# A fused Fourier transform and MLP kernel: the order of the weight conversions in its first chunk, and two transform parts placed at earlier steps

## The chip, the cores and the metric

The kernel runs on one core of a Trainium2 chip. The metric is the time of one execution on the device in microseconds; the kernel before has a median of 988.9 us over three runs (988.49 to 988.94). A lower time is better.

The core has five engines, each with its own queue of instructions that it works through in order: TensorE (matmuls; PE in the profile, and PEld for its weight loads), VectorE (DVE), ScalarE (ACT), GpSimd (POOL) and SyncE (SP, which here only issues DMAs). An instruction waits at the head of its queue until what it needs is there, and everything behind it on that engine waits too.

## The reference

```python
def _attn_ref(x):                       # x: 8 x 3136 x 256
    X = np.fft.fft(x, axis=1)
    X = np.fft.fft(X, axis=2)
    return X.real.astype(np.float32)

def _moe_ref(x, g_ln, w_ch1, w_ch2):    # w_ch1: 256 x 1024, w_ch2: 1024 x 256
    mu = np.mean(x, axis=-1, keepdims=True)
    var = np.mean((x - mu) ** 2, axis=-1, keepdims=True)
    xn = (x - mu) / np.sqrt(var + 1e-06) * g_ln
    ch = np.maximum(xn @ w_ch1, 0.0) @ w_ch2
    return (x + ch).astype(np.float32)
```

The output is `_moe_ref(_attn_ref(x), ...)`: the real part of a two-dimensional Fourier transform, and on its rows a normalised two-layer MLP with a residual.

## The kernel before

The long transform (3136 points) is done as matmuls in two steps. Step 1 multiplies folded input with a 64-point table and stores the result to a scratch tensor in DRAM; step 2, `step2(m, part)`, reads it back in another layout and multiplies it with a second table. A batch has 8 such parts m, so there are 64 in all. Each part makes 196 columns (tokens) of transformed data; the tokens are cut into chunks c of 256. A chunk's data exist three times: in full (`ck`), as a rounded high half (`ckh`) and as the rest (`ckl`), since products are made from three passes of halves. `step2` has its parts named by letters: "m" the matmuls (L311) into a PSUM bank, "h" the cast to the high half on ScalarE (L332), "f" the full copy on ScalarE (L334), "l" the subtraction for the low half on VectorE (L336). The bank is the single bank "fft", or "y" where a second part falls on the same step.

The MLP runs in steps s, eight to a chunk (s = 8c + f, f being a slice of 128 of the 1024 hidden columns):

- `moe1_a(s)`: six matmuls (L356) of the slice of w1 with the chunk into a PSUM bank of the pair "ab", so that s uses the bank of s-2; then a copy on ScalarE (`asb`, L361) and two adds on VectorE (L362 and L363, `h`). The second add is the last reader of the bank.
- `moe1_b(s)`: on ScalarE the rectified high half (`h_hi`, L370), on VectorE the low half (`h_lo`, L371). `h_lo` needs `h_hi`.
- `moe2(s)`: twelve matmuls (L406) of `h_hi` and `h_lo` with w2's halves, summed over the chunk's eight steps.

The main loop issues for each s: `moe1_b(s-1)`, `moe1_a(s)`, what is listed under "late" for s, `moe2(s-3)`, and what is listed under "after" for s (step 2 and 1 parts, residuals, stores). So VectorE's and ScalarE's queues hold what is "late" for s right behind the adds or the copy of s, and TensorE's queue holds the "after" matmuls behind `moe2(s-3)`. A table made at L619 to L629 gives each step 2 part m its s: eight steps for each chunk in which the part's first token lies, less 3; its "l" part is late at s+1. The steps before s = 6 are written out by hand (L767 to L813), mixed with the preparation of the weights.

The weights arrive as 64-bit integers (doubles) and are converted to float32 on the engines. For tile n of w2 (four tiles of two hidden slices each): `convert_m` is two VectorE instructions (L523, L525), `convert_z` one on ScalarE (L531), `convert_b` two on VectorE (L536, L538; it needs `convert_z`), `finish_w2` one on VectorE (L598). `split_w2` then casts the high half on ScalarE (L542) and subtracts for the low half on GpSimd (L543). Tile n is needed by `moe2` of f = 2n and 2n+1. w1 goes through a matmul as well (L576); its high half is cast by `round_w1`, its rest computed by `rest_w1` (L589) and cast by `rest_w1_copy` (L594), for columns 0 to 511 with k = 0 and for 512 to 1023 (used by s = 4 to 7 of a chunk) with k = 1.

TensorE begins with some warm-up matmuls (L683), does step 1 of the first batch, the matmuls of w1, more warm-up, and then `step2(0)` and `step2(1)`; `moe1_a(0)` starts 34 us into the span.

Of the kernel before, what the change touches and what calls it, by code (L numbers as in the profile page):

```python
# [32 lines left out]
CW = 256  # L33
# [113 lines left out]
def tile_kernel(ctx: ExitStack, tc: tile.TileContext, x, g_ln, w1, w2, tu, tab, tz, ty, tw, out):  # L147
# [139 lines left out]
    def first_token(m):  # L287
        b, j = divmod(m, 8)
        return b * REG + max(gb[2 * j] - 2, 0)
# [212 lines left out]
    def convert_a(key, wp):  # L502
        convert_m(key, wp)
        convert_z(key, wp)
# [24 lines left out]
    def convert_z(key, wp):  # L529
        high, e = conv[key][:2] if key in conv else convert_e(key, wp)  # L530
        nc.scalar.activation(e, high.bitcast(F32), AF.Copy, scale=2.0 ** -112)  # L531
# [13 lines left out]
    w1p, w2p = [], []  # L545
# [26 lines left out]
    def transform_w1(k, i):  # L572
        for j in range(2):
            if i == 0:
                psw[k, j] = psum.tile([128, 512], F32, tag=f"acc{k}", name=f"psw{k}{j}", bufs=2)
            nc.tensor.matmul(psw[k, j], tw_s[:, i, j], gws[2 * k + i], start=(i == 0),  # L576
                             stop=(i == 1))
# [14 lines left out]
    def rest_w1_copy(k):  # L592
        for j in range(2):
            nc.scalar.copy(w1_cols(w1_lo, k, j), psw.pop((k, j)))  # L594

    def finish_w2(n):
        _, e, f = conv.pop(f"w2_{n}")
        nc.vector.scalar_tensor_tensor(out=f, in0=f, scalar=2.0 ** -20, in1=e, op0=ALU.mult,  # L598
                                       op1=ALU.mult)
        return f  # L600

    def split_w2(n, f):
        split(w2_hi[:, 2 * n:2 * n + 2], w2_lo[:, 2 * n:2 * n + 2],
              f.rearrange("p (f d) -> p f d", f=2), nc.gpsimd)
# [10 lines left out]
    def add_late(s, fn, *args):  # L615

        late.setdefault(s, []).append((fn, args))

    first = {}  # L619
    for m in range(3, 64):  # L620
        s = 8 * (first_token(m) // CW) - 3
        if s in first:
            second.add(m)
        first.setdefault(s, []).append(m)
    for s, ms in first.items():
        for m in ms:
            add(s, step2, m, "mhf")
        for m in ms:
            add_late(s + 1, step2, m, "l")  # L629
    def behind(s):  # L630

        return s + 1 + (len(first[s]) > 1)
# [46 lines left out]
    def warm_up(n, zeros):  # L679

        pw = psum.tile([128, 2 * D], F32, tag="fft", name="pw")
        for i in range(n):
            nc.tensor.matmul(pw, zeros[:, :128], zeros, start=True, stop=True)  # L683

    E = mybir.EngineType
    with tc.manual_schedule(engines={E.PE, E.Activation, E.DVE, E.Pool}):
        with tc.manual_schedule(engines={E.SP}):
            nc.vector.memset(one, 1.0)
            for t in (warm, warm_h):
                nc.vector.memset(t, 0.0)  # L690
            for n, t in ((2, warm), (3, warm_h)):
                warm_up(n, t)
            nc.scalar.dma_start(tu_s, tu)
            load_x(0, 0)
            nc.scalar.activation(one, one, AF.Sqrt)
            for i in range(1, 5):
                load_x(0, i)
            load_w1(0)
            for i in (5, 6):
                load_x(0, i)  # L700
            nc.scalar.dma_start(g_s, g_ln.rearrange("(i p) -> p i", p=128))
            load_w1(1)
            nc.sync.dma_start(tw_all, tw)
            load_w1(2)
            load_w1(3)
            nc.gpsimd.memset(zmu, 0.0)
            nc.gpsimd.memset(masked, 0.0)
            ends(0, 0, 6)
            for i in range(3):
                fold_zw(0, i, nc.vector)  # L710
                step1(0, i)
            step1_ends(0, 0, 6)
            for i in range(3):
                store1(0, i, nc.scalar if i % 2 else nc.gpsimd)
            fold_zw(0, 3, nc.vector)
            step1(0, 3)
            ends(0, 6, 10)
            fold_zw(0, 4, nc.vector)
            convert_z("w1_0", w1p[0])
            convert_m("w1_0", w1p[0])  # L720
            step1(0, 4)
            step1_ends(0, 6, 10)
            store1(0, 3, nc.scalar)
            store1(0, 4, nc.gpsimd)
            fold_zw(0, 5, nc.vector)
            convert_b("w1_0")
            step1(0, 5)
            ends(0, 10, NS)
            fold_zw(0, 6, nc.vector)
            convert_z("w1_1", w1p[1])  # L730
            nc.vector.tensor_scalar_mul(g_s, g_s, 2.0 ** -20)
            finish_w1(0)
            convert_m("w1_1", w1p[1])
            step1_ends(0, 10, NS)
            store1(0, 5, nc.scalar)
            convert_b("w1_1")
            convert_z("w1_2", w1p[2])
            finish_w1(1)
            step1(0, 6)
            store1(0, 6, nc.gpsimd)  # L740
            load_w2(0, nc.gpsimd)
            nc.gpsimd.dma_start(tab_s[:, :, :gb[4]], tab[:, :, :gb[4]])
            nc.gpsimd.dma_start(tz_s, tz)
            load_w2(1, nc.gpsimd)
            convert_z("w1_3", w1p[3])
            convert_m("w1_2", w1p[2])
            convert_b("w1_2")
            finish_w1(2)
            relayout(0, 0, 2)
            relayout(0, 2, 4)  # L750
            relayout(0, 4, 8)
            nc.sync.dma_start(tab_s[:, :, gb[4]:gb[8]], tab[:, :, gb[4]:gb[8]])
            load_w2(2)
            relayout(0, 8, 16)
            nc.scalar.copy(minus, tw_all[:, 512:])
            transform_w1(0, 0)
            transform_w1(0, 1)
            round_w1(0)
            convert_m("w1_3", w1p[3])
            convert_b("w1_3")  # L760
            load_w2(3)
            nc.sync.dma_start(ty_s, ty)
            nc.sync.dma_start(tab_s[:, :, gb[8]:], tab[:, :, gb[8]:])
            for i in range(NU):
                load_x(1, i)
            finish_w1(3)
            transform_w1(1, 0)  # L767
            rest_w1(0)
            rest_w1_copy(0)
            transform_w1(1, 1)  # L770
            round_w1(1)
            convert_z("w2_0", w2p[0])
            convert_m("w2_0", w2p[0])
            convert_b("w2_0")
            split_w2(0, finish_w2(0))
            convert_m("w2_1", w2p[1])
            warm_up(10, warm_h)
            step2(0, "m")
            step2(0, "hl")
            step2(1, "m")  # L780
            step2(1, "hl", 0)
            convert_z("w2_1", w2p[1])
            convert_b("w2_1")
            moe1_a(0, ((1, 0), (0, 0), (0, 1)))
            moe1_a(1, ((1, 0), (0, 0), (0, 1)))
            rest_w1(1)
            moe1_b(0)
            step2(0, "f")
            moe1_a(2)
            f = finish_w2(1)  # L790
            moe1_b(1)
            split_w2(1, f)
            moe1_b(2)
            moe1_a(3)
            rest_w1_copy(1)
            step2(1, "f")
            convert_a("w2_2", w2p[2])
            step2(1, "hl", 1)
            moe2(0)
            moe1_b(3)  # L800
            moe1_a(4)
            convert_b("w2_2")
            f = finish_w2(2)
            nc.gpsimd.tensor_scalar(out=neg, in0=ty_s[:, 1, 129:130], scalar1=2.0, scalar2=-1.0,
                                    op0=ALU.mult, op1=ALU.add)
            moe2(1)
            step2(2, "m")
            moe1_b(4)
            split_w2(2, f)
            moe1_a(5)  # L810
            step2(2, "hf")
            step2(2, "l")
            convert_a("w2_3", w2p[3])  # L813
            moe2(2)
            add_late(6, convert_b, "w2_3")
            add_late(6, lambda: w2f.append(finish_w2(3)))
            add_late(7, lambda: split_w2(3, w2f.pop()))
            add_late(14, split, t1_hi, t1_lo, tu_s[:, 0:128])

        main.append(True)  # L820
        lag, last = 3, 8 * NCH
        for s in range(6, last):
            moe1_b(s - 1)
            moe1_a(s)
            for fn, args in late.get(s, ()):
                fn(*args)
            moe2(s - lag)
            for fn, args in after.get(s, ()):
                fn(*args)
        moe1_b(last - 1)  # L830
        inverse_std(LC)
        moe2(last - 3)
        for i, side in ((0, 0), (1, 0), (0, 1), (1, 1)):
            for t in (last - 2, last - 1):
                moe2(t, ((i, side),))
            finish_last(i, side)
# [18 lines left out]
```

## Time and profile before

| | us |
|---|---|
| median of three runs | 988.9 |
| the profiled execution | 988.67 |
| its span (first to last instruction) | 986.9 |
| TensorE busy | 976.8 |
| VectorE busy | 815.5 |
| ScalarE busy | 535.6 |
| GpSimd busy | 252.1 |

The profile is one execution taken by the hardware profiler. In its lists of instructions in order of time a row has the start within the span, the duration, the engine, the line of the kernel, the operation, output<-inputs by the program's names (buffer numbers left out), the shape, the number of instructions, and in brackets the idle time of the engine ahead of it and what ended that. Matmuls overlap in the pipeline, so that one lasts 0.28 us while they start 0.11 us apart. In the list of waits a row has the waiting engine and its line, what it waited for, and the time in total, how often, and the longest.

### The profile page before, as it was taken

How to read it: one execution, taken by the hardware profiler on the slowest of the kernel's cores; microseconds unless marked ns; L12 is line 12 of the kernel's file. 1: busy time of each engine (PE TensorE's matmuls, PEld its weight loads, DVE VectorE, ACT ScalarE, POOL GpSimd, SP SyncE). 2: the span in 40 equal slices, each digit the busy share in tenths (PEclk: the TensorE clock that was granted, in tenths of full speed). 3: DMA queues.
4: the chain of work that ended last, by engine and by line, in shares of the span. 5: the costliest groups of instructions: out<-in, count | busy, mean ns of one | idle time of the engine just before them, and what ended most of it. 6: DMA issues, size and time to landing. Idle time of an engine off the chain costs nothing.

```text
span 986.9 us, 22042 instructions
## 1 busy us (share of the span) xinstructions
PE 976.8 (99%) x8426; PEld 962.9 (98%) x8427; DVE 815.5 (83%) x2190; ACT 535.6 (54%) x1416; POOL 252.1 (26%) x282
## 2 busy tenths in 40 slices
PE   9899999999999999999999999999999999999998
PEld 6699999999999999999999999999999999999998
DVE  6888887888888888878888888888888888888887
ACT  3655655555555555555555556555555554555553
POOL 3247343224322332322342234223322300000000
PEclk9999999999999999999999999999999999999999
DMA  8924352215221252112521242212311112100101
GB/s 336 330 101 134 101 173 76 87 54 150 76 97 55 75 161 87 65 65 73 164 86 54 86 139 87 96 55 75 109 52 36 54 53 88 44 23 22 44 23 44
DMA packets 41161, 92.12 MB, mean 93 GB/s; under 512 B 4080, under 2 KB 18400, under 8 KB 40160
## 3 DMA queue, kind: packets, MB, share of 16 engines
q1 hardware_dynamic: 39088, 87.25, 26.7%
q0 software_dynamic: 736, 2.47, 0.7%
q8 instruction: 67, 1.10, 0.5%
q10 hardware_dynamic: 1232, 0.99, 0.3%
q14 instruction: 38, 0.31, 0.1%
HBM read 50.32 MB, written 40.37 MB: 92 GB/s over the span
## 4 chain that ended last, share of the span: by engine, by line
PE 91%; DVE 7%; ACT 2%; issue 1%; ACTq 0%; DVEq 0%
PE acc L406 50%; PE ab L356 25%; PE ps L311 6%; PE psy L431 4%; PE ps L263 3%; DVE h_lo L371 2%; DVE h L362 1%; DVE h L363 1%; PE pw L683 1%; ACT h_hi L370 1%; DVE ew L538 0%; PE ps L255 0%; PE ps L257 0%; DVE fw L525 0%; DVE st L453 0%
## 5 line engine op out<-in xcount | busy, mean ns | idle before, releaser
L406 PE MATMUL acc<-w_hi,h_lo 128*128 128x256 f32 x1568 | 433.2, 276 | 0.2 <-DVE h_lo L371 0.2
L406 PE MATMUL acc<-w_hi,h_hi 128*128 128x256 f32 x1568 | 433.0, 276 | 0.0
L406 PE MATMUL acc<-w_lo,h_hi 128*128 128x256 f32 x1568 | 433.0, 276 | 0.0
L371 DVE SCALAR_TENSOR_TENSOR h_lo<-h,h_hi 128x512 fp32r<-128x512 f32 x392 | 294.1, 750 | 141.2 <-ACT h_hi L370 138.8
L370 ACT ACTIVATE h_hi<-h 128x512 fp32r<-128x512 f32 x392 | 250.0, 638 | 292.9 <-DVE h L363 292.9
L406 PEld LDWEIGHTS acc<-w_hi,h_lo 128*128 128x128 f32 x1568 | 294.3, 188 | 0.6 <-DVE h_lo L371 0.4
L406 PEld LDWEIGHTS acc<-w_hi,h_hi 128*128 128x128 f32 x1568 | 294.4, 188 | 0.0
L406 PEld LDWEIGHTS acc<-w_lo,h_hi 128*128 128x128 f32 x1568 | 294.4, 188 | 0.0
L356 PE MATMUL ab<-ckl,w_hi 128*128 128x256 f32 x768 | 218.0, 284 | 2.3 <-DVE h L363 2.3
L356 PE MATMUL ab<-ckh,w_lo 128*128 128x256 f32 x768 | 212.7, 277 | 2.0 <-ACT w_lo L594 1.7
L356 PE MATMUL ab<-ckh,w_hi 128*128 128x256 f32 x768 | 212.1, 276 | 0.0
L225 POOL TENSOR_TENSOR fl<-f,fh 128x512 fp32r<-128x512 f32 x49 | 64.0, 1306 | 504.9 <-ACT fh L219 494.2
L362 DVE TENSOR_TENSOR h<-asb,ab 128x256 f32<-128x256 f32 x384 | 158.7, 413 | 0.5 <-ACT asb L361 0.5
L363 DVE TENSOR_TENSOR h<-asb,ab 128x256 f32<-128x256 f32 x384 | 158.9, 414 | 0.0
L356 PEld LDWEIGHTS ab<-ckl,w_hi 128*128 128x128 f32 x768 | 144.2, 188 | 3.5 <-issue 1.9
L356 PEld LDWEIGHTS ab<-ckh,w_lo 128*128 128x128 f32 x768 | 144.3, 188 | 2.5 <-ACT w_lo L594 1.9
L356 PEld LDWEIGHTS ab<-ckh,w_hi 128*128 128x128 f32 x768 | 144.2, 188 | 0.0
L361 ACT COPY asb<-ab 128x256 f32<-128x256 f32 x384 | 137.9, 359 | 8.9 <-PE ab L356 1.2
L267 ACT COPY s<-ps 128x508 f32<-128x508 f32 x56 | 32.8, 586 | 62.6 <-PE ps L263 50.7
L311 PE MATMUL ps<-tab_s,s 112*128 112x98 f32 (+1 forms) x512 | 65.6, 273 | 0.1
L311 PEld LDWEIGHTS ps<-tab_s,s 112*128 112x128 f32 x512 | 61.8, 191 | 0.6 <-PE pw L683 0.6
L332 ACT CAST ckh<-ps 128x392 fp32r<-128x392 f32 (+49 forms) x112 | 39.7, 356 | 39.7 <-PE ps L311 39.5
(111 smaller groups left out, 980.2 us busy)
## 6 DMA issues: line engine op xcount, KB each, us to landing
xs<-x SPq DMA_DIRECT2D x56, 512.0 KB, 4.1
out<-o SPq DMA_DIRECT2D x96, 256.0 KB, 2.0
scratch<-s SPq DMA_DIRECT2D x49, 256.0 KB, 2.3
s<-scratch SPq DMA_DIRECT2D x7, 1792.0 KB, 9.8
w1p_all<-w SPq DMA_DIRECT2D x6, 512.0 KB, 8.9
scratch<-s POOLq DMA_DIRECT2D x4, 256.0 KB, 6.0
w1p_all<-w POOLq DMA_DIRECT2D x2, 512.0 KB, 5.2
s<-scratch SPq DMA_DIRECT2D x1, 896.0 KB, 10.9
```

The lines of the kernel that those rows point to most:

```text
L225: nc.gpsimd.tensor_tensor(out=lo, in0=f, in1=hi.bitcast(F32), op=ALU.subtract)
L267: nc.scalar.copy(s[:, :, :, :127], ps[:, :, :, :127])
L311: nc.tensor.matmul(ps[:, h, k0 - base:k1 - base], s2[b][:KP, g, 128 * h:128 * h + 128], tab_s[:, h, k0:k1], start=(h == 0 and g == 2 * j), ...
L332: nc.scalar.copy(hi, src)
L356: nc.tensor.matmul(pt, wt[wi][:, j, fs], ch[xi][:, j, :w], start=(n == 0), stop=(n == 2))
L361: nc.scalar.copy(asb[:, :w], pa)
L362: nc.vector.tensor_tensor(out=h[:, :w], in0=asb[:, :w], in1=pb, op=ALU.add)
L363: nc.vector.tensor_tensor(out=h[:, w:], in0=asb[:, :m], in1=pb[:, :m], op=ALU.subtract)
L370: nc.scalar.activation(h_hi, h, AF.Relu)
L371: nc.vector.scalar_tensor_tensor(out=h_lo, in0=h, scalar=0.0, in1=h_hi.bitcast(F32), op0=ALU.max, op1=ALU.subtract)
L406: nc.tensor.matmul(acc[c, i][:, side], hs[xi][:, h0:h0 + 128], ws[wi][:, f], start=(f == 0 and side == 0 and n == 0), stop=(f == 7 and n = ...
L431: nc.tensor.matmul(ps[:, j, :n], ck[:, j], ty_s[:, j, :n], start=(j == 0), stop=True, skip_group_check=True)
```

## The change

In the written-out part the conversions of w2's tiles are put in another order between the other work: `convert_z` of tile 0 ahead of `transform_w1(1, 1)` and `round_w1(1)`; all of tile 1's conversion ahead of `step2(0)`, its finish ahead of `moe1_a(0)` and its split behind it; tile 2 begun behind `moe1_b(0)`; the finish of tile 3 late at step 7 and no longer at 6. `rest_w1_copy(1)` goes ahead of `moe1_b(1)`, the full copies of step2(0) and step2(1) further back. In the table step2(3) goes from step 13 to 7 (its "l" part from 14 to 10), step2(4) from 21 to 10 (its "l" from 22 to 14). Step2(5) stays at 21; as it is alone there now, it uses bank "fft" and not "y". The instructions themselves and their number stay the same, and so does TensorE's order apart from the two moved parts.

```diff
@@ the table of step 2 parts
-        s = 8 * (first_token(m) // CW) - 3
+        s = {3: 7, 4: 10}.get(m, 8 * (first_token(m) // CW) - 3)
...
         for m in ms:
-            add_late(s + 1, step2, m, "l")
+            add_late({3: 10, 4: 14}.get(m, s + 1), step2, m, "l")
@@ the steps written out
             rest_w1_copy(0)
+            convert_z("w2_0", w2p[0])
             transform_w1(1, 1)
             round_w1(1)
-            convert_z("w2_0", w2p[0])
             convert_m("w2_0", w2p[0])
             convert_b("w2_0")
             split_w2(0, finish_w2(0))
+            convert_z("w2_1", w2p[1])
             convert_m("w2_1", w2p[1])
+            convert_b("w2_1")
             warm_up(10, warm_h)
...
             step2(1, "hl", 0)
-            convert_z("w2_1", w2p[1])
-            convert_b("w2_1")
+            f = finish_w2(1)
             moe1_a(0, ((1, 0), (0, 0), (0, 1)))
+            split_w2(1, f)
             moe1_a(1, ((1, 0), (0, 0), (0, 1)))
             rest_w1(1)
             moe1_b(0)
+            convert_m("w2_2", w2p[2])
+            moe1_a(2)
+            rest_w1_copy(1)
+            moe1_b(1)
+            moe1_a(3)
+            convert_z("w2_2", w2p[2])
+            convert_b("w2_2")
             step2(0, "f")
-            moe1_a(2)
-            f = finish_w2(1)
-            moe1_b(1)
-            split_w2(1, f)
             moe1_b(2)
-            moe1_a(3)
-            rest_w1_copy(1)
+            moe2(0)
             step2(1, "f")
-            convert_a("w2_2", w2p[2])
             step2(1, "hl", 1)
-            moe2(0)
+            moe1_a(4)
+            f = finish_w2(2)
             moe1_b(3)
-            moe1_a(4)
-            convert_b("w2_2")
-            f = finish_w2(2)
...
             moe2(1)
+            split_w2(2, f)
             step2(2, "m")
             moe1_b(4)
-            split_w2(2, f)
...
             add_late(6, convert_b, "w2_3")
-            add_late(6, lambda: w2f.append(finish_w2(3)))
+            add_late(7, lambda: w2f.append(finish_w2(3)))
```

The instructions below are named line, operation, output<-inputs, shape; the number after a name is that of the step, chunk, tile or part (`h_hi7` is the high half of step 7, `fw2_3` tile 3 of w2, `ps2_3` the bank of step2(3), `psw10` the bank of w1's rests), and a last one only numbers the buffer.

The first place is ScalarE's queue around the casts of w1's rests (L594), before:

```order
L361 COPY asb2_391<-ab2_384 128x256
L370 ACTIVATE h_hi1_397<-h1_372 128x512
L542 CAST w2_hi_73<-fw2_1_314 128x512
L370 ACTIVATE h_hi2_403<-h2_392 128x512
L361 COPY asb3_414<-ab3_407 128x256
L594 CAST w1_lo_77<-psw10_289 128x512
L594 CAST w1_lo_77<-psw11_291 128x512
```

and there now:

```order
L542 CAST w2_hi_73<-fw2_1_315 128x512
L361 COPY asb1_374<-ab1_367 128x256
L370 ACTIVATE h_hi0_381<-h0_361 128x512
L361 COPY asb2_397<-ab2_390 128x256
L594 CAST w1_lo_77<-psw10_289 128x512
L594 CAST w1_lo_77<-psw11_291 128x512
L370 ACTIVATE h_hi1_404<-h1_375 128x512
L361 COPY asb3_415<-ab3_408 128x256
```

The casts of the rests now stand right behind the copy of step 2, and the cast of w2's tile 1 ahead of the copy of step 1.

The second place is VectorE's queue at the end of step 6 and in step 7, around the finish of tile 3 (L598), before:

```order
L538 SCALAR_TENSOR_TENSOR ew2_3_509<-w1p_all_93,ew2_3_509 128x512
L598 SCALAR_TENSOR_TENSOR fw2_3_511<-fw2_3_511,ew2_3_509 128x512
L371 SCALAR_TENSOR_TENSOR h_lo6_566<-h6_540,h_hi6_565 128x512
L362 TENSOR_TENSOR h7_577<-asb7_576,ab7_569 128x256
L363 TENSOR_TENSOR h7_577<-asb7_576,ab7_569 128x256
L371 SCALAR_TENSOR_TENSOR h_lo7_602<-h7_577,h_hi7_601 128x512
```

and there now:

```order
L538 SCALAR_TENSOR_TENSOR ew2_3_509<-w1p_all_93,ew2_3_509 128x512
L371 SCALAR_TENSOR_TENSOR h_lo6_565<-h6_540,h_hi6_564 128x512
L362 TENSOR_TENSOR h7_576<-asb7_575,ab7_568 128x256
L363 TENSOR_TENSOR h7_576<-asb7_575,ab7_568 128x256
L598 SCALAR_TENSOR_TENSOR fw2_3_511<-fw2_3_511,ew2_3_509 128x512
L371 SCALAR_TENSOR_TENSOR h_lo7_614<-h7_576,h_hi7_613 128x512
```

The finish moved behind the low half of step 6 and both adds of step 7. ScalarE's queue at the same place, from the cast of tile 3 (L542) on, before:

```order
L542 CAST w2_hi_73<-fw2_3_511 128x512
L370 ACTIVATE h_hi7_601<-h7_577 128x512
L361 COPY asb8_612<-ab8_605 128x256
L370 ACTIVATE h_hi8_639<-h8_613 128x512
L361 COPY asb9_650<-ab9_643 128x256
```

and there now:

```order
L542 CAST w2_hi_73<-fw2_3_511 128x512
L332 CAST ckh2_485<-ps2_3_601 128x2x181
L334 COPY ck2_484<-ps2_3_601 128x2x181
L332 CAST ckh3_609<-ps2_3_601 128x2x15
L334 COPY ck3_608<-ps2_3_601 128x2x15
L370 ACTIVATE h_hi7_613<-h7_576 128x512
L361 COPY asb8_624<-ab8_617 128x256
```

Between the cast of tile 3 and the high half of step 7 now stand the four copies of step2(3).

The third place is VectorE's queue in step 10, before:

```order
L371 SCALAR_TENSOR_TENSOR h_lo9_679<-h9_651,h_hi9_678 128x512
L362 TENSOR_TENSOR h10_690<-asb10_689,ab10_682 128x256
L363 TENSOR_TENSOR h10_690<-asb10_689,ab10_682 128x256
L371 SCALAR_TENSOR_TENSOR h_lo10_711<-h10_690,h_hi10_710 128x512
L362 TENSOR_TENSOR h11_722<-asb11_721,ab11_714 128x256
```

and there now:

```order
L371 SCALAR_TENSOR_TENSOR h_lo9_691<-h9_663,h_hi9_690 128x512
L362 TENSOR_TENSOR h10_702<-asb10_701,ab10_694 128x256
L363 TENSOR_TENSOR h10_702<-asb10_701,ab10_694 128x256
L336 TENSOR_TENSOR ckl2_486<-ps2_3_601,ckh2_485 128x2x181
L336 TENSOR_TENSOR ckl3_610<-ps2_3_601,ckh3_609 128x2x15
L371 SCALAR_TENSOR_TENSOR h_lo10_732<-h10_702,h_hi10_731 128x512
```

The two subtractions of step2(3) stand behind the adds of step 10; on TensorE the matmuls of step2(4) stand at the end of the same step, behind `moe2(7)` and ahead of `moe1_a(11)`.

## The prediction

> **What bounds the kernel now.** I read the page first, then busy time by stretch, then the waits of TensorE, then each engine's instructions in order of time. Two lines of the page:
>
> ```profile
> span 986.9 us, 22042 instructions
> PE 976.8 (99%) x8426; PEld 962.9 (98%) x8427; DVE 815.5 (83%) x2190; ACT 535.6 (54%) x1416; POOL 252.1 (26%) x282
> ```
>
> The profiled execution took 988.67 us, 1.77 more than its span; the median of the runs is 988.9. TensorE works 99% of the span. Two stretches (length, then busy time of PE, PEld, DVE, ACT, POOL, then the granted clock) and the two waits of TensorE in the first of them:
>
> ```profile
> 34.00:90.00 56.00, 52.06 (x437) 50.53 (x437) 48.92 (x119) 32.92 (x88) 26.38 (x31) 1.00 0.51 172
> 90.00:986.90 896.90, 893.41 (x7871) 892.23 (x7869) 744.02 (x2025) 488.77 (x1302) 216.88 (x234) 1.00 0.24 80
> ```
>
> ```profile
> PE ab L356 <- DVE h L363: 2.3, 6, 0.8
> PE ab L356 <- ACT w_lo L594: 1.7, 1, 1.7
> ```
>
> From 34 to 90 us TensorE idles 3.94 us, and these two waits make it up. Everything that the change touches lies there, so its waits can give back 3.9 us at most, 0.4%. Six of seven waits are for VectorE's second add (L363): the bank pair "ab" holds two steps, so moe1_a(s) cannot start before VectorE is done with s-2. VectorE sets the pace here, TensorE later. TensorE's places:
>
> ```profile
> 41.25 0.39 PE L356 MATMUL ab<-ckh,w_lo 128*128 128x256 f32 x1 [1.68 <-ACT w_lo L594]
> 60.07 0.36 PE L356 MATMUL ab<-ckl,w_hi 128*128 128x256 f32 x1 [0.49 <-DVE h L363]
> 62.60 0.36 PE L356 MATMUL ab<-ckl,w_hi 128*128 128x256 f32 x1 [0.23 <-DVE h L363]
> 62.91 0.28 PE L356 MATMUL ab<-ckh,w_hi 128*128 128x256 f32 x1
> 66.78 1.03 PE L311 MATMUL ps<-tab_s,s 112*128 112x98 f32 x8
> 67.59 0.37 PE L356 MATMUL ab<-ckl,w_hi 128*128 128x256 f32 x1
> 87.40 1.92 PE L311 MATMUL ps<-tab_s,s 112*128 112x98 f32 x16
> 89.16 1.08 PE L431 MATMUL psy<-ty_s,ck 128*128 128x130 f32 x8
> 90.00 0.37 PE L356 MATMUL ab<-ckl,w_hi 128*128 128x256 f32 x1
> ```
>
> 60.07 is moe1_a(11), 66.78 is step2(3), 87.40 step2(4) and step2(5), 90.00 moe1_a(22). From there TensorE does the same in both kernels without waiting for this stage, so the change of the time is the shift of that last row. I work it out backwards: what TensorE has to do up to it, and when it can begin.
>
> **TensorE's side of the two moved parts.** From 60.07 to 90.00 are 29.93 us. In the changed kernel this lacks step2(3) (66.78 to 67.59, 0.81), step2(4) (half of 87.40 to 89.16, 0.88), the wait of 0.23, and two restarts, whose first matmul lasts 0.37 against 0.28 (0.18 together): 27.83 are left. Ahead of it now stands step2(4), 0.81. If T is when step2(4) starts, moe1_a(22) starts at T + 28.64.
>
> T is not free. Step2(3) and step2(4) use the same single PSUM bank "fft". The last reader of step2(3) is its "l" part, two subtractions (L336) on VectorE, now queued behind the adds of step 10. Behind the waiting step2(4) stand moe1_a(11) and all of TensorE's work. So VectorE has to be followed to the end of these two. VectorE's rows (start, duration), then those of ScalarE and GpSimd:
>
> ```profile
> 34.98 0.69 DVE L538 SCALAR_TENSOR_TENSOR ew<-w1p_all,ew 128x512 int32<-128x512 int32 x1
> 35.59 0.41 DVE L362 TENSOR_TENSOR h<-asb,ab 128x256 f32<-128x256 f32 x1
> 36.59 0.42 DVE L363 TENSOR_TENSOR h<-asb,ab 128x256 f32<-128x256 f32 x1
> 37.04 0.69 DVE L371 SCALAR_TENSOR_TENSOR h_lo<-h,h_hi 128x512 fp32r<-128x512 f32 x1
> 37.91 0.42 DVE L362 TENSOR_TENSOR h<-asb,ab 128x256 f32<-128x256 f32 x1 [0.18 <-ACT asb L361]
> 39.18 0.68 DVE L371 SCALAR_TENSOR_TENSOR h_lo<-h,h_hi 128x512 fp32r<-128x512 f32 x1
> 40.48 1.33 DVE L371 SCALAR_TENSOR_TENSOR h_lo<-h,h_hi 128x512 fp32r<-128x512 f32 x1 [0.61 <-ACT h_hi L370]
> 41.73 0.41 DVE L362 TENSOR_TENSOR h<-asb,ab 128x256 f32<-128x256 f32 x1
> 45.59 0.69 DVE L538 SCALAR_TENSOR_TENSOR ew<-w1p_all,ew 128x512 int32<-128x512 int32 x1
> 46.32 0.69 DVE L598 SCALAR_TENSOR_TENSOR fw<-fw,ew 128x512 f32<-128x512 f32 x1
> 46.92 0.69 DVE L371 SCALAR_TENSOR_TENSOR h_lo<-h,h_hi 128x512 fp32r<-128x512 f32 x1
> 47.97 0.42 DVE L362 TENSOR_TENSOR h<-asb,ab 128x256 f32<-128x256 f32 x1 [0.36 <-ACT asb L361]
> 54.53 0.42 DVE L363 TENSOR_TENSOR h<-asb,ab 128x256 f32<-128x256 f32 x1
> 55.64 0.83 DVE L371 SCALAR_TENSOR_TENSOR h_lo<-h,h_hi 128x512 fp32r<-128x512 f32 x1 [0.70 <-ACT h_hi L370]
> 62.04 0.41 DVE L363 TENSOR_TENSOR h<-asb,ab 128x256 f32<-128x256 f32 x1
> 72.07 0.62 DVE L336 TENSOR_TENSOR ckl<-ps,ckh 128x362 fp32r<-128x362 f32 x2
> ```
>
> ```profile
> 35.06 0.38 ACT L361 COPY asb<-ab 128x256 f32<-128x256 f32 x1 [0.57 <-PE ab L356]
> 39.30 0.62 ACT L542 CAST w_hi<-fw 128x512 fp32r<-128x512 f32 x1 [0.89 <-DVE fw L598]
> 39.82 0.62 ACT L370 ACTIVATE h_hi<-h 128x512 fp32r<-128x512 f32 x1
> 54.98 0.63 ACT L370 ACTIVATE h_hi<-h 128x512 fp32r<-128x512 f32 x1 [0.65 <-DVE h L363]
> 68.16 0.46 ACT L332 CAST ckh<-ps 128x362 fp32r<-128x362 f32 x1
> 68.94 0.22 ACT L334 COPY ck<-ps 128x30 f32<-128x30 f32 x1
> 39.99 1.27 POOL L543 TENSOR_TENSOR w_lo<-fw,w_hi 128x512 fp32r<-128x512 f32 x1 [5.54 <-ACT w_hi L542]
> ```
>
> **VectorE up to step 7.** The conversions of w2's second tile now fill VectorE's idle time ahead of step2(0), and its finish (L598) stands ahead of the first add. TensorE's first moe1_a does not move: it waits for step2(0) behind the warm-up. The first add no longer follows an L538, only its copy: 35.06 + 0.38 + 0.03 = 35.47, not 35.59. From 35.59 to the second add of step 7 (54.53) took 18.94. Out of it go: two L598 of 0.60 (46.32 to 46.92), one now ahead, one behind, 1.20; two places where L598 waited for its L538 (0.73 from 45.59 to 46.32, against 0.61 from 34.98 to 35.59), 0.24; and the gaps beyond the usual slot (0.33 for an add, 0.60 for L371): 0.12 before 37.04, 0.27 before 37.91, 0.70 before 40.48, 0.65 before 41.73, 0.45 before 47.97, together 2.19. New gaps come in: the cast of tile 1 (L542, 0.52 to the next) stands ahead of the second copy, 0.10. GpSimd's subtraction of tile 1 meets h_lo(0): the row at 40.48 shows what that does, it ended 0.55 after GpSimd's row at 39.99 ended and lasted 1.33; here 0.24 by the times. And that whole pattern (0.70 for an h_hi behind L542, 0.65 for GpSimd) now falls on h_lo(4), behind tile 2's cast: 1.35. Sum 18.94 - 1.20 - 0.24 - 2.19 + 1.69 = 17.00: the second add of step 7 at 52.47, a lead of 2.06 us.
>
> **The lead is spent in step 7.** The finish of tile 3 (due at 7 now, not 6) starts at 52.80 and ends at 53.49. Its cast on ScalarE starts at 53.52, 0.52. Next on ScalarE stand four copies of the moved step2(3): 68.16 to 68.94 and 0.12 more, 0.90. Only then h_hi(7): 54.94, against 54.98 before. VectorE idles two microseconds for it and starts h_lo(7) at 55.60, where it was before. GpSimd's part of tile 3 also ends later (53.52 + 0.62 + 0.05 + 1.27 = 55.46), and moe2(6) waits for it; VectorE, not this, sets T.
>
> **Step 10.** From 55.64 to 62.04 VectorE's list is unchanged: second add of step 10 at 62.00, then 0.33 to the "l" part, 0.62 for the pair (72.07): 62.95. TensorE starts 0.15 after such an end (62.45 to 62.60): T = 63.10, moe1_a(22) at 91.74, **1.74 later**. TensorE had been ready since about 59.4 (the add of step 8 at about 57.1, 18 matmuls and a restart 2.1), so one wait of some 3.7 us stands where 0.49 and 0.23 stood. On ScalarE h_hi(10) stands behind the copies of step2(4) and is late too; moe2(10), which needs it, comes three steps (6 us) later, which covers it.
>
> [...] The longest wait above is 1.68, and the granted clock stayed at 1.00. [...]
>
> **Edits without a term.** The 1.68 at 41.25 goes, since the casts of w1's rests now follow the copy of step 2 and not that of step 3; next late is the add of step 2, behind two conversions of tile 2. That gain is real at 41 us but not at T. Tile 2 is converted from about 37.8 on; its load:
>
> ```profile
> 27.73 0.51 SPq L557 DMA_DIRECT2D w1p_all<-w  x1
> w1p_all<-w SPq DMA_DIRECT2D x1, 512.0 KB, 8.5
> ```
>
> lands at 36.2, 1.6 ahead; without that cover VectorE would wait and T with it. Step2(5) goes from bank "y" to "fft", free since step 14: nothing. The moved parts issue no DMA, and no queue of SP changes.
>
> **Bounds.** GpSimd's meetings (0.24, 0.65) may be missing or double, 0.9 either way: the forecast is 0.9 to 2.7 us later, 989.8 to 991.6.
>
> **Rivals.** (A) Slower: in the wait of 3.7 us the clock is halved. If it lasts for as long as the wait, TensorE loses half of that, 1.85: 992.5. It decides once a wait lies over a limit somewhere above 1.68; against it speaks the 1.00 in every stretch. (B) VectorE's lead lasts: without the GpSimd meetings and the delay of h_lo(4) (1.59) and with 0.4 less in the chain of step 7, T is 2.0 earlier: -0.3, 988.6. For it speaks that the meetings hang on tenths; against it ScalarE's fixed queue. (C) Faster: step2(4) does not wait for "l". Then it fits into the wait for the add of step 9, moe1_a(11) starts at 60.03, moe1_a(22) at 87.86, 2.1 earlier: 986.8. Against it speaks the single bank.
>
> **The numbers.** Forecast 0.73, A 0.10, B 0.10, C 0.07. What a measurement can tell from no change is 0.2%, 1.98 us; I put 0.44 of the forecast's 0.73 below it, 0.29 above. Slower 0.29 + 0.10 = 0.39, same 0.44 + 0.10 = 0.54, faster 0.07. Likeliest 988.9 + 1.7 = 990.6. The range goes from B, 988.6, to 992.0, above the forecast's bound by part of A.
>
> **What would show it.** Right: no wait at moe1_a(4) for L594; VectorE idle about 2 us ahead of h_lo(7), released by L370; moe2(6) waiting for L543; an L311 at about 63 waiting 3 to 4 us for L336. Wrong: that wait under 2 us, h_lo(7) well ahead of 55, or a granted clock under 1.00 near 63.

## The result and the profile after

The changed kernel takes 992.13 us (median of 12 runs, 990.68 to 993.27), the kernel before 989.12 us in the same measurement: ratio 1.0024, 95% interval 1.0015 to 1.0032. A second measurement (the experiment "the changed kernel again") gave 992.17 against 989.16, ratio 1.0033, interval 1.0021 to 1.0046. The change makes the kernel slower by 0.24 to 0.33%, some 2.4 to 3.3 us; by the medians it is 3.0 us both times. The forecast was 990.6 us, 1.7 more than 988.9, with bounds of 0.9 and 2.7 more and a range of 988.6 to 992.0. So its direction came true, and the loss of 3.0 us lies above its bounds, at the upper end of the range. The median of 992.13 is 0.13 us beyond that end, but the kernel before, too, took 0.22 us more here than the 988.9 from which the forecast counts. The ratios below leave out two slow executions of the kernel with the moves alone (1022.10 and 2556.20 us of its 12); its median counts them and is 992.4 us without them.

The profiled execution of the changed kernel took 993.27 us. Its span and busy times, and the two stretches that the prediction looked at (length, then busy time of PE, PEld, DVE, ACT, POOL, then the granted clock):

```profile
span 991.5 us, 22046 instructions
PE 978.2 (99%) x8426; PEld 965.3 (97%) x8427; DVE 816.5 (82%) x2190; ACT 536.3 (54%) x1416; POOL 252.0 (25%) x282
```

```profile
34.00:90.00 56.00, 50.45 (x399) 48.71 (x399) 44.75 (x108) 29.45 (x79) 22.75 (x26) 0.94 0.48 161
90.00:991.50 901.50, 898.01 (x7912) 896.83 (x7910) 748.87 (x2038) 492.88 (x1310) 220.10 (x237) 1.00 0.24 80
```

From 34 to 90 us TensorE now idles 5.55 us (56.00 - 50.45) where it idled 3.94, and the granted clock of that stretch is 0.94 where it was 1.00. Both losses lie there. The place where the two kernels meet again, moe1_a(22), starts at 94.62 here (90.00 before), and from it to the end are 896.88 us (896.90 before): nothing is lost or won later.

TensorE's waits from 34 to 100 us, and its rows at the wait and behind it:

```profile
PE ps L311 <- issue: 3.5, 1, 3.5
PE acc L406 <- POOL w_lo L543: 1.0, 1, 1.0
PE ab L356 <- DVE h L363: 0.2, 1, 0.2
```

```profile
56.64 0.38 PE L406 MATMUL acc<-w_lo,h_hi 128*128 128x256 f32 x1 [0.96 <-POOL w_lo L543]
...
64.01 2.00 PE L311 MATMUL ps<-tab_s,s 112*128 112x98 f32 x8 [3.46 <-issue]
65.71 0.56 PE L356 MATMUL ab<-ckl,w_hi 128*128 128x256 f32 x1
66.07 0.41 PE L356 MATMUL ab<-ckh,w_lo 128*128 128x256 f32 x1
66.28 0.41 PE L356 MATMUL ab<-ckh,w_hi 128*128 128x256 f32 x1
...
94.62 0.37 PE L356 MATMUL ab<-ckl,w_hi 128*128 128x256 f32 x1
```

Of the six short waits for VectorE's adds one of 0.21 us is left, and the 1.68 us for L594 have gone. In their place stands one wait of 3.46 us ahead of step2(4) at 64.01. The profile puts it down to "issue": the releaser that the prediction named (L336) isn't printed, and experiments had to settle it. Behind the wait, step2(4) itself takes 1.70 us (64.01 to 65.71) where 0.81 was the price, and matmuls start 0.21 us apart (66.07 to 66.28) where 0.11 is usual. The granted clock says why:

```profile
62.00:64.00 2.00, 0.00 (x0) 0.02 (x1) 1.91 (x6) 0.20 (x1) 0.05 (x1) 0.64 0.00 0
64.00:66.00 2.00, 1.99 (x9) 2.00 (x10) 0.00 (x0) 0.00 (x0) 0.00 (x0) 0.50 0.00 0
66.00:68.00 2.00, 2.00 (x12) 2.00 (x11) 0.52 (x1) 1.76 (x4) 0.00 (x0) 0.50 0.03 8
68.00:70.00 2.00, 2.00 (x13) 2.00 (x13) 1.86 (x9) 0.63 (x1) 0.00 (x0) 0.65 0.00 0
```

TensorE is fully busy from 64 us on, but at half the clock until about 69.4. A stretch of 2 us at 0.64 has 1.44 us of half clock in it if the rest is at 1.00 (2 x 0.36 x 2.00, since time at half clock lowers the mean by half of its share), so the four rows make 1.44 + 2.00 + 2.00 + 1.40 = 6.84 us.

In this execution step2(0) had to wait 0.9 us for its data, which it did not in the profiled execution of the kernel before, and everything behind it starts later. The second measurement's profile starts as before's did (first moe1_a at 34.01, against 33.97), so its times can be laid beside the prediction's directly. VectorE and TensorE there:

```profile
52.47 0.41 DVE L363 TENSOR_TENSOR h<-asb,ab 128x256 f32<-128x256 f32 x1
52.80 0.69 DVE L598 SCALAR_TENSOR_TENSOR fw<-fw,ew 128x512 f32<-128x512 f32 x1
55.59 0.69 DVE L371 SCALAR_TENSOR_TENSOR h_lo<-h,h_hi 128x512 fp32r<-128x512 f32 x1 [2.11 <-ACT h_hi L370]
61.86 0.41 DVE L363 TENSOR_TENSOR h<-asb,ab 128x256 f32<-128x256 f32 x1
62.19 0.62 DVE L336 TENSOR_TENSOR ckl<-ps,ckh 128x362 fp32r<-128x362 f32 x2
```

```profile
62.92 1.10 PE L311 MATMUL ps<-tab_s,s 112*128 112x98 f32 x8 [3.52 <-issue]
93.38 0.36 PE L356 MATMUL ab<-ckl,w_hi 128*128 128x256 f32 x1
```

The second add of step 7 stands at 52.47, its low half at 55.59 behind 2.11 us of idle VectorE, the second add of step 10 at 61.86, and step2(4) starts right behind the "l" part, at 62.92. Only the last row is off: 93.38, where the prediction had 91.74.

### The profile page after: what moved, and what is told of

It reads as the page before. It is cut to its first block, busy times and chain, and to the rows that moved or that the text cites. A ratio compares the mean times of both kernels' runs of the same rounds, so it can differ in the third digit from the quotient of the medians.

```text
span 991.5 us, 22046 instructions
## 1 busy us (share of the span) xinstructions
PE 978.2 (99%) x8426; PEld 965.3 (97%) x8427; DVE 816.5 (82%) x2190; ACT 536.3 (54%) x1416; POOL 252.0 (25%) x282
## 4 chain that ended last, share of the span: by engine, by line
PE 92%; DVE 3%; issue 2%; ACT 1%; POOL 1%; DMA 1%; POOLq 0%; DVEq 0%; ACTq 0%
PE acc L406 52%; PE ab L356 26%; PE ps L311 5%; PE psy L431 4%; PE ps L263 3%; DVE h_lo L371 1%; DMA w1p_all<-w 1%; PE pw L683 0%; DVE h L362 0%; DVE h L363 0%; ACT h_hi L370 0%; POOL scratch L271 0%; PE ps L257 0%; PE ps L255 0%; POOL w_lo L543 0%
```

## The experiments

All ratios are to the kernel before, timed in the same measurement, with a 95% interval. T is the start of step2(4) in the profiled execution, "idle" TensorE's idle time ahead of it, and "left" the time from T to moe1_a(22).

| kernel | median, us | ratio | T | idle | moe1_a(22) | left |
|---|---|---|---|---|---|---|
| changed | 992.13 | 1.0024 (1.0015 to 1.0032) | 64.01 | 3.46 | 94.62 | 30.61 |
| changed, again | 992.17 | 1.0033 (1.0021 to 1.0046) | 62.92 | 3.52 | 93.38 | 30.46 |
| order only | 988.04 | 0.9989 (0.9979 to 1.0000) | at step 21 | - | 90.61 | - |
| moves only | 993.20 | 1.0042 (1.0024 to 1.0059) | 63.20 | 3.54 | 92.88 | 29.68 |
| "l" at 8 | 987.70 | 0.9987 (0.9977 to 0.9997) | 59.80 | 0 | 90.01 | - |
| own bank | 988.00 | 0.9986 (0.9977 to 0.9996) | 59.00 | 0 | 88.42 | - |
| filled wait | 990.99 | 1.0020 (1.0009 to 1.0032) | 67.28 | 0.93 | 96.23 | 28.95 |
| filled wait, again | 990.39 | 1.0013 (1.0005 to 1.0022) | 63.59 | 0.92 | 92.13 | 28.54 |
| finish at 6 | 990.82 | 1.0016 (1.0005 to 1.0027) | 61.40 | 3.30 | 92.08 | 30.68 |
| "l" at 8, finish at 6 | 987.74 | 0.9984 (0.9975 to 0.9993) | 57.76 | 0 | 87.62 | - |

**The two halves of the change, each alone.** First the new order of the conversions, with the two moved parts put back:

```diff
-        s = {3: 7, 4: 10}.get(m, 8 * (first_token(m) // CW) - 3)
+        s = 8 * (first_token(m) // CW) - 3
...
-            add_late({3: 10, 4: 14}.get(m, s + 1), step2, m, "l")
+            add_late(s + 1, step2, m, "l")
```

> The changed kernel with its two moved parts put back (step2(3) at step 13, step2(4) at step 21, each 'l' part one step later); the new order of w2's conversions stays. Theory W (the loss is the new wait of step2(4) for the bank 'fft', near 64 us, and the halved clock behind it): no L311 that waits over 1 us between 55 and 75 us, granted clock 1.00 from 60 to 90 us, time 0 to 1.5 us under the kernel before (ratio 0.999). Rival C (the loss comes with the conversions: step2(0) starts 0.9 us later, tile 3's finish is a step later): as slow as the changed kernel, ratio to the kernel before about 1.002.

Measured: ratio 0.9989 (0.9979 to 1.0000), and no wait for step2(4) in the stretch; the longest there is moe2(6)'s wait of 1.0 us for L543. The granted clock:

```profile
60.00:75.00 15.00, 14.64 (x125) 14.31 (x124) 12.93 (x35) 8.66 (x27) 7.56 (x9) 1.00 0.30 106
```

So the conversions cost nothing; they may save a microsecond. The rival C of that text (the loss comes with the conversions) falls. Then the same two lines the other way round, put into the kernel before:

```diff
-        s = 8 * (first_token(m) // CW) - 3
+        s = {3: 7, 4: 10}.get(m, 8 * (first_token(m) // CW) - 3)
...
-            add_late(s + 1, step2, m, "l")
+            add_late({3: 10, 4: 14}.get(m, s + 1), step2, m, "l")
```

> The kernel before with the two moved parts alone (step2(3) at 7, step2(4) at 10, their 'l' parts at 10 and 14); the conversions stay in the order of before. Theory W: step2(4) waits 2.5 to 5 us for the 'l' part of step2(3), the granted clock falls to about half for some 5 us behind it, ratio to the kernel before 1.002 to 1.005. Rival C: without the new conversion order there is nothing to lose, ratio 1.000 or under.

Measured: ratio 1.0042 (1.0024 to 1.0059). Its row of step2(4), and the mean clock behind it:

```profile
63.20 1.10 PE L311 MATMUL ps<-tab_s,s 112*128 112x98 f32 x8 [3.54 <-issue]
```

```profile
60.00:75.00 15.00, 11.80 (x90) 11.83 (x91) 11.38 (x32) 6.61 (x16) 6.12 (x7) 0.89 0.25 91
```

The moved parts carry the whole loss: the same wait and the same fall of the clock, without any of the reordered conversions. 1.0042 x 0.9989 = 1.0031 is the whole change, within its two intervals.

**What step2(4) waits for.** The profile says "issue"; the prediction said the "l" part of step2(3), which keeps the bank. Two kernels take that apart. In the one, the "l" part comes earlier:

```diff
-            add_late({3: 10, 4: 14}.get(m, s + 1), step2, m, "l")
+            add_late({3: 8, 4: 14}.get(m, s + 1), step2, m, "l")
```

> The changed kernel with one number changed: the 'l' part of step2(3), the last reader of the bank, is issued in step 8 and not in step 10. Theory W: step2(4) finds its bank free and waits under 1 us, granted clock 1.00 from 60 to 90 us, time 0 to 1.5 us under the kernel before (ratio 0.999). Rival V (VectorE sets moe1_a(11) and what follows anyway, with or without the wait at the bank): the wait moves to an L356 behind it, with the same sum, ratio 1.002.

Measured: ratio 0.9987 (0.9977 to 0.9997). VectorE's "l" part and TensorE's step2(4):

```profile
57.43 0.62 DVE L336 TENSOR_TENSOR ckl<-ps,ckh 128x362 fp32r<-128x362 f32 x2
```

```profile
59.80 1.03 PE L311 MATMUL ps<-tab_s,s 112*128 112x98 f32 x8
```

The bank is free at about 58.05, TensorE comes to step2(4) at 59.80 and does not wait. Rival V falls too: what is left for the adds are tenths (1.2 us over four waits), not the 3.5 us. In the other, step2(4) gets a bank of its own:

```diff
-            ps2[m] = psum.tile([128, 2, CW], F32, tag="y" if m in second else "fft", name=f"ps2_{m}")
+            ps2[m] = psum.tile([128, 2, CW], F32, tag="y" if m in second or m == 4 else "fft", name=f"ps2_{m}")
```

> The changed kernel with step2(4)'s sums in bank 'y' and not in 'fft', which step2(3) still holds; nothing else. Theory W: step2(4) no longer waits for the 'l' part of step2(3); the wait of 3.5 us at its L311 falls under 1 us, the granted clock stays 1.00 from 60 to 90 us, ratio to the kernel before 0.998 to 1.000. The prediction's third rival (step2(4) fits into the wait for the add of step 9) gives 2.1 us less than the kernel before, ratio 0.998. Rival Y (bank 'y' has readers of its own there): the wait comes back at the same place for another line, ratio 1.001 or more.

Measured: ratio 0.9986 (0.9977 to 0.9996), with the "l" part where the change put it:

```profile
59.00 1.03 PE L311 MATMUL ps<-tab_s,s 112*128 112x98 f32 x8
59.81 0.37 PE L356 MATMUL ab<-ckl,w_hi 128*128 128x256 f32 x1
```

```profile
61.54 0.62 DVE L336 TENSOR_TENSOR ckl<-ps,ckh 128x362 fp32r<-128x362 f32 x2
```

Step2(4) starts 2.5 us ahead of that "l" part. Rival Y falls. Together the two kernels show the releaser that the profile does not print: the last reader of the bank. One small edit in either place turns a loss of 2.4 to 3.3 us into a gain of about 1.3 by the ratios, 0.7 to 0.9 by the medians.

**What the wait costs, and what the clock.** Here TensorE gets something to do in the wait, ahead of step2(4):

```diff
+    def filler(n):
+        pw = psum.tile([128, 2 * D], F32, tag="y", name="pwf")
+        for i in range(n):
+            nc.tensor.matmul(pw, warm_h[:, :128], warm_h, start=True, stop=True)
...
+            if m == 4:
+                add(s, filler, 12)
```

> The changed kernel with 12 more matmuls (bf16, 128x256, of the warm-up's operand into the bank 'y') just ahead of step2(4) in step 10, so that TensorE works through a part of its wait; what they compute is not used. Theory W with both parts (the wait and the halved clock): step2(4) starts where it starts in the changed kernel, 63.5 to 64.2 us, its own wait is 1 to 2.5 us, the granted clock stays 1.00 behind it, and moe1_a(22) starts 1.5 to 2.5 us earlier than the changed kernel's 94.62: ratio to the kernel before 1.000 to 1.001. Rival H (the halved clock costs nothing at the end, since VectorE sets the pace behind it): moe1_a(22) and the time as in the changed kernel, ratio 1.002 to 1.003.

The filler's matmuls are 128x512, not 128x256 as that text has it; they take 2.76 us. Measured: ratio 1.0020 (1.0009 to 1.0032), on rival H's side by the ratios of that text. It does not tell the theories apart: the changed kernel's own ratio of 1.0024 comes from another measurement, and this profile has a disturbance of its own at its start (last section). So both were run once more, on one chip:

> The changed kernel itself once more, beside the next one on the same chip. Both theories: ratio to the kernel before 1.002 to 1.003; in its profile one wait of 3 to 4 us at the L311 of step2(4) and a granted clock of 0.50 for some 5 us behind it.

> The changed kernel with 12 matmuls of the warm-up's operand (bf16, 128x512) ahead of step2(4) once more, beside the changed kernel on the same chip. Theory W with both parts: 1 to 2 us under the changed kernel's median, granted clock 1.00 from 50 to 90 us, moe1_a(22) 28.3 to 29.0 us behind the start of step2(4), against 30.6 in the changed kernel. Rival H (the halved clock costs nothing): the same time as the changed kernel, within 0.5 us.

Measured: 992.17 us (1.0033) for the changed kernel, 990.39 us (1.0013) with the wait filled, 1.78 us less. The filled kernel's rows and clock, and the changed kernel's clock:

```profile
63.59 1.10 PE L311 MATMUL ps<-tab_s,s 112*128 112x98 f32 x8 [0.92 <-PE pwf L623]
92.13 0.37 PE L356 MATMUL ab<-ckl,w_hi 128*128 128x256 f32 x1
```

```profile
60.00:75.00 15.00, 14.02 (x112) 12.44 (x113) 11.38 (x32) 6.16 (x15) 6.56 (x8) 1.00 0.27 94
```

```profile
60.00:75.00 15.00, 12.08 (x90) 12.12 (x91) 11.38 (x31) 6.73 (x16) 5.82 (x7) 0.89 0.22 82
```

Against the first moe1_a, step2(4) starts hardly earlier for the filler (28.76 us behind it, against 28.91), but from it to moe1_a(22) are 28.54 us, against 30.46. By the medians 1.8 us are the clock; the other 1.3 us (1.0013) are the wait, net of what the conversions give. Rival H falls: the clock is paid for at the end. The division is that of this measurement: in the first one the filled kernel was 2.4 us above the kernel before (990.99 against 988.60), here 1.2 (990.39 against 989.16).

By the profiles, the 1.92 us between 30.46 and 28.54 are not quite like with like. The first and the last start of the twelve matmuls of a moe2, first in the changed kernel's second profile, then in the filled kernel:

```profile
72.47 0.28 PE L406 MATMUL acc<-w_hi,h_lo 128*128 128x256 f32 x1
73.77 0.28 PE L406 MATMUL acc<-w_hi,h_hi 128*128 128x256 f32 x1
```

```profile
74.34 0.28 PE L406 MATMUL acc<-w_hi,h_lo 128*128 128x256 f32 x1
75.58 0.28 PE L406 MATMUL acc<-w_hi,h_hi 128*128 128x256 f32 x1
```

Eleven starts take 1.30 us in the one and 1.24 in the other, both at a granted clock of 1.00; what decides this was not found. The first profile with the filled wait (28.95) has the wider spacing too, and the other three with the unfilled wait have the closer one. Like with like, 3.40 us of half clock cost 1.51 us (30.46 - 28.95) or 1.14 (29.68 of the moves alone - 28.54), and the 6.84 us of the other two profiles cost 2.07 and 2.14 (30.61 and 30.68 - 28.54). With the closer spacing, twice the time at half clock costs 1.8 to 1.9 times as much.

The other executions bear this out. Of the changed kernel's 12, nine have a granted clock of 0.998 over the whole span, which is what 3.40 us of half clock make of it, and take 991.56 us in the mean; three have 0.996 or 0.997, as 6.84 us make it, and take 992.98. Of the 12 with the finish at 6 (below), five have 0.998 and take 990.28, six have 0.996 and take 991.37. So the 1.8 us by the medians are a mixture of executions with some 3.4 us of half clock and with some 6.8. Where in the span the clock fell is known for the profiled ones alone, and it matters: in the measurement of the moves alone, the kernel before has 0.998 in ten of 35 executions and is no slower in them (988.84 us in the mean, against 988.80 in the 18 with 1.00).

**How long a wait has to be.** Waits of several lengths were put into the kernel before:

```diff
+    def stall(k):
+        for i in range(k):
+            nc.vector.tensor_tensor(out=warm_h, in0=warm_h, in1=warm_h, op=ALU.max)
+    def probe():
+        pw = psum.tile([128, 2 * D], F32, tag="y", name="pwp")
+        nc.tensor.matmul(pw, warm_h[:, :128], warm_h, start=True, stop=True)
+    for i, k in enumerate((4, 8, 12, 16, 20, 24, 32, 40)):
+        add_late(81 + 48 * i, stall, k)
+        add(81 + 48 * i, probe)
```

> The kernel before with eight waits of TensorE put in, 48 steps apart (steps 81 to 417): in each, 4, 8, 12, 16, 20, 24, 32 or 40 idle operations on VectorE (128x512, bf16, in place), and behind them one matmul that needs the last. What that matmul computes is not used. Theory G (a gate): short waits leave the granted clock at 1.00; from a length between 1.7 us (no fall in the kernel before) and 3.5 us (fall in the changed kernel) on, the clock is 0.50 for a time that does not depend on the length, 4 to 7 us, and each such wait costs 2 to 3 us beyond itself. Rival P (in proportion): each wait lowers the clock, for about as long as it lasted: the shorter ones for 2 us, the longest for over 10 us.

The eighth place lies behind the last step (there are 384), so there are seven waits. One execution was taken, of 1065.93 us. TensorE's waits, the shortest of the seven, and the clock around its end:

```profile
PE pwp L638 <- DVE warm_h L633: 45.3, 6, 12.2
PE ab L356 <- DVE warm_h L633: 15.5, 1, 15.5
```

```profile
238.64 0.61 PE L638 MATMUL pwp<-warm_h 128*128 128x512 bf16 x1 [3.03 <-DVE warm_h L633]
```

```profile
238.00:240.00 2.00, 1.36 (x6) 1.27 (x7) 1.16 (x3) 0.00 (x0) 0.00 (x0) 0.60 0.94 272
240.00:242.00 2.00, 2.00 (x12) 2.00 (x12) 0.94 (x4) 0.56 (x2) 0.00 (x0) 0.55 0.88 229
```

The two rows make 1.60 + 1.80 = 3.40 us of half clock, 3.16 of them behind the wait's end. All seven, by such rows:

| wait, us | 3.03 | 4.61 | 6.45 | 8.56 | 10.40 | 12.24 | 15.45 |
|---|---|---|---|---|---|---|---|
| half clock in all | 3.40 | 3.40 | 6.80 | 10.24 | 10.24 | 13.64 | 17.08 |
| of it behind the wait's end | 3.16 | 3.38 | 4.80 | 4.62 | 5.17 | 3.64 | 4.79 |

In the five longer waits 2.00 to 12.29 us of the half clock lie ahead of the wait's end. What is left of it behind the end is 3.2 to 5.2 us and does not grow with the length: theory G holds against rival P, though not quite with the 4 to 7 us expected. The span is 77.3 us longer than before's, the seven waits are 60.8 us of it, so each costs 2.4 us beyond itself. Of these 16.5 us, half of the 29.56 us of half clock behind the ends makes 14.8; what the rest is was not taken apart. All seven were long enough, so this kernel does not show which length is too short; the shortest with a half clock is 3.03 us.

**Where VectorE's lead goes.** The prediction had it spent in step 7, behind the finish of tile 3:

```diff
-            add_late(7, lambda: w2f.append(finish_w2(3)))
+            add_late(6, lambda: w2f.append(finish_w2(3)))
```

> The changed kernel with the finish of w2's fourth tile issued in step 6 and not in step 7; nothing else. The prediction's account of step 7 (finish, cast, then four copies of step2(3) ahead of h_hi(7)): the cast comes earlier, VectorE's idle time ahead of h_lo(7) falls from 2.1 to 0.8 to 1.3 us, moe2(6) no longer waits for L543, step2(4) starts 0.8 to 1.3 us earlier against moe1_a(0), but its wait stays near 3.5 us with the halved clock behind it: ratio 1.001 to 1.002. Rival Z (the copies alone make h_hi(7) late, the finish has no part in it): idle time 2.1 us and start as in the changed kernel, ratio 1.0025.

Measured: ratio 1.0016 (1.0005 to 1.0027). VectorE and TensorE:

```profile
54.23 0.69 DVE L371 SCALAR_TENSOR_TENSOR h_lo<-h,h_hi 128x512 fp32r<-128x512 f32 x1 [0.84 <-ACT h_hi L370]
```

```profile
61.40 2.00 PE L311 MATMUL ps<-tab_s,s 112*128 112x98 f32 x8 [3.30 <-issue]
92.08 0.37 PE L356 MATMUL ab<-ckl,w_hi 128*128 128x256 f32 x1
```

The idle time ahead of h_lo(7) falls from 2.11 to 0.84, moe2(6)'s wait is gone, and step2(4) comes 1.26 us earlier against the first moe1_a (27.65 us behind it, 28.91 in the changed kernel's second profile). The wait stays 3.30 us and so does the halved clock, for twice as long in this execution (0.77 over 60 to 75 us). Rival Z falls. So the account of step 7 holds, and mending it alone does not mend the kernel.

**Both mends together.** The "l" part at 8 and the finish at 6, two numbers of the changed kernel:

```diff
-            add_late({3: 10, 4: 14}.get(m, s + 1), step2, m, "l")
+            add_late({3: 8, 4: 14}.get(m, s + 1), step2, m, "l")
...
-            add_late(7, lambda: w2f.append(finish_w2(3)))
+            add_late(6, lambda: w2f.append(finish_w2(3)))
```

> The changed kernel with the 'l' part of step2(3) issued in step 8 (as in the run where it was 10 to 8) and the finish of w2's fourth tile issued in step 6 again, not 7. Theory W: no wait at step2(4); the finish no longer stands behind the second add of step 7, so the cast comes earlier, VectorE's idle time of 2.1 us ahead of h_lo(7) shrinks to under 1 us, moe2(6) no longer waits for GpSimd's L543, and the kernel is 1 to 2 us under the kernel before (ratio 0.998). Rival B (VectorE's rate alone sets the pace there, wherever the finish stands): as with the 'l' part alone, ratio 0.9987, no better.

Measured: 987.74 us, ratio 0.9984 (0.9975 to 0.9993), faster than both kernels. Its profile:

```profile
span 984.5 us, 22047 instructions
```

```profile
34.00:90.00 56.00, 54.39 (x457) 53.01 (x456) 48.96 (x121) 34.16 (x94) 27.51 (x31) 1.00 0.54 181
```

TensorE idles 1.61 us in the stretch where it idled 3.94 before and 5.55 with the change: 2.3 us of the 3.9 that could be had. moe1_a(22) stands at 87.62, 2.38 us ahead of before's. Whether it beats the "l" part alone (0.9987) the ratios don't tell: 0.9984 lies within that interval, and the rival B of that text (VectorE's rate alone sets the pace) is not shut out by them. The traces are against it: step2(4) comes at 57.76 and not at 59.80, and this profile's start is about 0.9 us earlier, so 1.1 us of it belong to the finish.

## Why the prediction was right on the wait and too low on its cost

**VectorE up to step 7: right.** The sum of 17.00 us put the second add at 52.47; it stands at 52.47 in the comparable profile. That it fits to the hundredth is luck: the first add starts at 35.63 and not at 35.47, and the way from there took 16.84 us and not 17.00. The two meetings with GpSimd are there: in the first profile h_lo(0) lasts 0.94 us, and h_lo(4) starts after 0.62 us of idle time and lasts 1.35. The wait for L594 at 41 us is gone.

**The lead is spent in step 7: right.** h_lo(7) was put at 55.60 behind two microseconds of idle VectorE; it stands at 55.59 behind 2.11. moe2(6) waits for L543, 0.96 us. The kernel with the finish at 6 shows the cause by taking part of it away.

**Step 10 and T: right.** Add at 62.00, measured 61.86; T at 63.10, measured 62.92; a wait of some 3.7 us, measured 3.52. What releases it is the "l" part, as the kernels with an earlier "l" part and with another bank show.

**T + 28.64: right at full clock, and here the forecast fell short.** With the wait filled, 28.54 us were measured (28.95 in the other profile), at a granted clock of 1.00 from 60 to 75 us. Without the filler they are 30.61 and 30.46. The forecast's 1.74 us have nothing in them for the clock; the runs show 1.1 to 1.5 us more for 3.40 us of half clock and 2.1 us more for 6.84. The halved clock stood in the prediction as rival A, at a price of 1.85 and a time of 992.5 us. That a wait halves the clock was a supposition there, and no run had shown it: the longest wait in the rows of before, 1.68 us, left the clock at 1.00. The experiments show 0.50, and a loss of 1.1 to 2.1 us in place of the 1.85. Measured were 992.13 and 992.17. That A's price comes so near has luck in it: A let the half clock last as long as the wait, and this wait of 3.5 us is about as long as one stretch of 3.40; behind the waits of 6.45 to 15.45 us it lasted 3.6 to 5.2. The range, too, reaches to 992.0 only by "part of A". What was wrong is the chance of 0.10. It rested on "against it speaks the 1.00 in every stretch", but every stretch with 1.00 held no wait over 1.68 us, and the forecast's own wait was 3.7. The rows said nothing about a wait that long, and they were counted as if they did.

**The wait without the clock** was forecast as 1.7 us; the kernel with the filled wait, which is the change without the halved clock, took 1.2 us more than the kernel before by the medians, 1.3 by the ratio. **The prediction's rival B** (VectorE's lead lasts) did not happen: the second add of step 7 stood where the sum with GpSimd's meetings put it, and h_lo(7) was late. **Its rival C** (no wait at the bank) did not happen either, for the reason given against it, the single bank. With that taken away it comes near in the profile, moe1_a(11) at 59.81 where C put it at 60.03 and moe1_a(22) at 88.42 where C had 87.86, but the gain is 0.7 us by the medians and 1.4 by the ratio (0.9986), not 2.1.

**Edits without a term: right.** The order of the conversions, alone, measures as no loss (0.9989).

## What to carry to other kernels

A matmul moved to an earlier step needs its bank as early: look up who reads the bank last and move that reader as well, or give the matmul another bank; here one number or the other bank did it (ratios of 0.9987 and 0.9986, where the change as it was has 1.0024). When a sum predicts a wait on TensorE that is longer than any in the trace, the trace's clock of 1.00 is no evidence for that wait: price the halved clock as part of the wait (here 1.1 to 2.1 us on top of 1.3, at a wait of 3.3 to 3.5), not as an outside chance. And when a profile names "issue" for a long wait, take away the suspected reader in an experiment; the name alone settles nothing.

## What the hardware showed that was not expected

The half clock lasted 3.40 us in the changed kernel's second profile, with the moves alone and at the waits of 3.03 and 4.61 us; 6.80 to 6.84 us, twice that, in the changed kernel's first profile, in the one with the finish at 6, in the first with the filled wait and at the wait of 6.45 us; 10.24 us, three times 3.41, at the waits of 8.56 and 10.40 us; 13.64 at that of 12.24; and 17.08, five times 3.42, at the longest (15.45 us). It did not begin at a set time: in these profiles the clock fell 2.0 us (the changed kernel's first profile) to 5.3 us (the wait of 10.40 us) after TensorE had stopped. The same kernel had 6.84 us of it in one execution and 3.40 in another: in the first profile the clock fell 1.45 us ahead of the wait's end, in the second only 1.7 us after work had begun again:

```profile
62.00:64.00 2.00, 1.08 (x9) 1.11 (x10) 0.81 (x3) 0.00 (x0) 0.00 (x0) 1.00 0.00 0
64.00:66.00 2.00, 2.00 (x14) 2.00 (x13) 0.51 (x1) 1.66 (x4) 0.00 (x0) 0.66 0.03 8
66.00:68.00 2.00, 2.00 (x12) 2.00 (x11) 1.86 (x9) 0.63 (x1) 0.00 (x0) 0.50 0.00 0
```

The waits of 3.30 us (the finish at 6) and 3.03 us had a half clock as well, and between 1.67 and 1.90 us the outcome differed. In the first profile with the filled wait, TensorE waited 1.90 us for the data of step2(0), and then had half the clock for 6.84 us (four rows: 1.00 + 2.00 + 2.00 + 1.84); in the second, it waited 1.67 us at the same place and kept 1.00, as the changed kernel's first profile did behind a wait of 1.71 us at 22.39. The wait of 1.90 us, and the clock behind it:

```profile
33.80 0.66 PE L311 MATMUL ps<-tab_s,s 112*128 112x99 f32 x4 [1.90 <-DMA s<-scratch]
```

```profile
34.00:36.00 2.00, 2.00 (x16) 2.00 (x15) 1.93 (x5) 0.48 (x1) 0.00 (x0) 0.75 1.06 272
36.00:38.00 2.00, 1.65 (x8) 1.40 (x8) 1.35 (x4) 0.26 (x1) 0.00 (x0) 0.50 1.13 293
38.00:40.00 2.00, 2.00 (x11) 2.00 (x11) 0.77 (x3) 0.89 (x2) 0.17 (x1) 0.50 0.95 233
40.00:42.00 2.00, 2.00 (x10) 1.81 (x10) 1.47 (x5) 0.91 (x2) 1.12 (x1) 0.54 1.02 299
```

Whether a limit lies between 1.71 and 1.90 us was not tried.
